# Token routing through expert-sorted DRAM lists in place of one-hot tables, and seven-product arithmetic in all first expert blocks

## The chip, the cores and the metric

The kernel runs on one core of one Trainium2 chip. The metric is the device time of one execution in microseconds (us). A core has a matrix engine (TensorE, PE in the profile; PEld is its weight load), a vector engine (VectorE, DVE), an activation engine (ScalarE, ACT), a general engine (GpSimd, POOL) and a sequencer that issues DMAs (SyncE, SP). Each engine runs its own instruction stream in order and waits on semaphores for the others. In this program the large loads are issued by SP, and the gathers, the scatters and the stores of attention by POOL; all of them share 16 DMA engines.

## The reference

Sliding-window causal attention (8 batches, 8 heads, 576 positions, head size 64, window 64) gives 4608 tokens of 512 features. They go through a mixture of 8 experts with a locality gate, in float32:

```python
logits = x @ w_gate                       # [8, 576, 8]
local_gate = sigmoid(x @ w_local)
for b in range(B):
    prev_e = -1
    for s in range(S):
        fresh_e = argmax(logits[b, s])
        e = fresh_e if s == 0 or local_gate[b, s] < 0.5 else prev_e
        prev_e = e
        p = softmax(logits[b, s])
        h = relu(x[b, s] @ w1[e])         # 512 -> 1024
        out[b, s] = p[e] * (h @ w2[e])    # 1024 -> 512
```

So a token either takes its own best expert or that of the token before it. Which tokens an expert gets is known only once attention is done, and a part of them as soon as the first batches are.

## The kernel before

**Attention** (`attention`, L166) walks over 9 groups of 512 tokens (`sc`), each in 4 head pairs (`hp`): 36 units. A unit is scores (L383), an exponential on ACT (L414), a mask product on DVE (L419), and products with the values (L429), which DVE scales into `x` (L434 to L439). POOL stores `x` to the DRAM tensor `xs` after each group (L529). The gate logits of a group come to `lt`. The order of PE, ACT and SP is the written order here; that of DVE and POOL is chosen by the framework's scheduler. Twice in each unit `step` (L457) takes the next piece of a generator that emits routing work; each piece says by its yield how long it pauses.

**Routing** (`Router`) has two parts. Part 0 is the first three batches (14 chunks of 128 tokens), part 1 the other 23 chunks. `gate` (L766) finds each token's expert by a scan over the tokens, which passes through six small TensorE transposes or sums and back, and ranks the tokens of each expert. Then one-hot tables are built: for each chunk DVE makes `rowh` (128 x 128) and `colh` (128 x 5 x slots) in bf16 (`table`, L926), and one PE product for each chunk (L954) adds them into a table that says, for each slot of 128 rows, which token stands in which row and with what weight. `first` (L970) does part 0 within attention and yields three full blocks of 256 tokens; `second` (L1002) does part 1 after attention.

**Experts** (`Experts.run`, L1402) then works through blocks. `order` has 3 first blocks (-1, -2, -3), 13 blocks of 256 tokens, 4 of 128, 2 of 64 and 2 of 32. `weights` (L1137) reads the block's expert number into a register of SP and loads 2 MB of `w1` and 2 MB of `w2` into a ring of 4 buffers; `rows` (L1114) gathers the block's tokens from `xs` by indirect DMA. `turn` (L1150) transposes the tokens on PE. A *fast* block of 256 tokens uses seven products of quarter matrices instead of eight (`big_hidden` L1192, `big_result` L1244); the sums and differences of quarters that this needs are made on DVE (`left`, `right`, L1171 and L1180): four of `w1`, four of `x`, four of `w2`, four of `h`. Blocks -1 and -2 are listed as `PLAIN` (L73) and take the plain form: L1351 for the hidden layer, L1383 for the result. During these two blocks only PE's order is written out; DVE works off `second`, one piece after some products (`step`, L1417). From block -3 on the order of PE, DVE and ACT is the written one. Block 3 of `order` and all after it depend on `second`.

Of the kernel before, what the change touches and what calls it, by code (L numbers as in the profile page):

```python
# [1 line left out]

# [6 lines left out]
F32 = mybir.dt.float32  # L9
# [25 lines left out]
PIECE = 10  # L35
T1 = 3 * S
CUT = T1 % P
PART = slice(0, T1 // P + 1), slice(T1 // P, C)
C1 = PART[0].stop
CV = C + 1  # L40
CMAX = max(p.stop - p.start for p in PART)
FB = 3
FIRST = 2 * FB
assert CUT and CUT % 32 == 0
LEFT = N - FB * BIG
HF = P // 2
NB = (N + E * (HF - 1)) // BIG
SM0 = NB * 2
HF0 = SM0 + E
NS = HF0 + E  # L50
QR = P // 4
KINDS = NB, NB + E, NB + 2 * E
NBLK = KINDS[-1] + E
SURE = (LEFT + E * HF) // BIG - E // 2, E // 2, E // 4, E // 4
ZR = 16 * P
assert ZR >= T1
# [13 lines left out]
STEP = 3.5  # L70
LEAD = 2
MID = (KB, KB - 1)
PLAIN = (-1, -2)  # L73
# [8 lines left out]
def kernel(  # L82
# [23 lines left out]
    tabs = dict(idx=const.tile([P, NS], U32, name="idx"), pw=const.tile([P, NS], F32, name="pw"),  # L106
                ej=const.tile([1, NBLK + 1], I32, name="ej"), idxh=const.tile([P, E], U32, name="idxh"),
                pwh=const.tile([P, E], F32, name="pwh"),
                idxq=const.tile([P, E], U32, name="idxq"), pwq=const.tile([P, E], F32, name="pwq"), idx1=const.tile([P, FIRST], U32, name="idx1"),
                pw1=const.tile([P, FIRST], F32, name="pw1"), ej1=const.tile([1, FB], I32, name="ej1"),  # L110
                gx=const.tile([P, NS], U32, name="gx"), gx1=const.tile([P, FIRST], U32, name="gx1"))
# [9 lines left out]
    moe = xs, w1, w2, out, tabs, lt, ident  # L121
    with ExitStack() as fast:
        ring = fast.enter_context(tc.tile_pool(name="ring", bufs=4))
        rt = Router(fast, tc, lt, tabs, ident)
# [5 lines left out]
        attention(tc, ring, kq, v3, v4, vt, vh, xs, lt, ok, wgs, wg2s, ident, rt, ex)  # L130
        ex.run(fast, rt, lambda ps: flag(nc, ps, ok, bad, tabs["ej"][:, NBLK:], rare, ident))
    if_rare = nc.values_load(rare[0:1, 0:1], min_val=0, max_val=1,  # L132
                             skip_runtime_bounds_check_because="the larger of two comparisons")
    with tc.If(if_rare > 0):
        if_bad = nc.values_load(bad[0:1, 0:1], min_val=0, max_val=1,
                                skip_runtime_bounds_check_because="the result of a comparison")
        with tc.If(if_bad > 0):
            careful(tc, q, k, v, xs, lt, wgs, ident)
            with ExitStack() as slow:
                ring = slow.enter_context(tc.tile_pool(name="ring2", bufs=4))  # L140
                rt = Router(slow, tc, lt, tabs, ident)
                rt.prepare()
                ex = Experts(slow, tc, ring, *moe)
                with tc.tile_pool(name="rt_ps1", bufs=1, space=PSUM) as ps:
                    for _ in rt.first(lambda: ps.tile([P, SC], F32, name="a")):
                        pass
                ex.begin()
                ex.run(slow, rt)
        if_more = nc.values_load(tabs["ej"][0:1, NBLK:], min_val=0, max_val=1,
# [16 lines left out]
def attention(ctx, tc, ring, kq, v3, v4, vt, vh, xs, lt, ok, wg, wg2, ident, rt, ex):  # L166
# [290 lines left out]
    def step(free=True):  # L457
# [3 lines left out]
        if side and pause <= 0.0 and (free or not trip):  # L461
            w, trip = next(side, (0.0, None))
            pause = max(pause, -HALF) + w
            if trip is None:
                side = ()
                if ex.jobs:
                    ex.rows(ex.jobs[0], -1)
# [1067 lines left out]
```

## Time and profile before

| | |
|---|---|
| three timed runs | 653.6, 653.32, 650.35 us; median 653.32 us |
| the profiled execution | 656.34 us, span of the core 654.3 us |
| granted TensorE clock | 0.994 of full speed |
| busy, share of the span | PE 625.4 us (96%), PEld 538.5 us (82%), DVE 402.2 us (61%), ACT 182.6 us (28%), POOL 124.4 us (19%) |
| DMA | 165.78 MB, 253 GB/s on average |
| attention ends on PE, the first product of block -1 begins | 139.1 us |
| first product of block -3 | 205.1 us |
| first product of the fourth block | 231.9 us |

Times in a profile count from the first instruction of the profiled execution. A row of a timeline gives the start, the time taken, the engine, the line of the kernel and the operation with `out<-in`; in brackets is the time that the engine stood idle before it and who ended the wait. A row of the table of stretches gives the length of a stretch, then the busy time (and instructions) of each engine, the granted clock, the busy share of the DMA engines and the rate.

### The profile page before, as it was taken

What the parts mean: (1) busy time and instruction counts of PE and PEld (TensorE: products, weight loads), DVE (VectorE), ACT (ScalarE), POOL (GpSimd) and SP (SyncE); (2) the same over time, 40 slices, a digit from 0 to 9 for tenths busy, and PEclk for the clock granted to TensorE, in tenths of its full rate; (3) what the DMA queues carried; (4) which work ended last, traced back from release to release, by engine and by line L of the source; (5) the groups of instructions that cost most, each with busy time, mean ns of one, the idle gap of its engine ahead of it and who ended that gap; (6) DMA issues with size and microseconds to landing.
All of it is one profiled execution on the core that took longest, in us unless ns stands there. A gap on an engine that the chain in (4) does not pass through costs nothing. (4 is left out here: it accounts for less than half of the span.)

```text
span 654.3 us, 14680 instructions
## 1 busy us (share of the span) xinstructions
PE 625.4 (96%) x6307; PEld 538.5 (82%) x6307; DVE 402.2 (61%) x742; ACT 182.6 (28%) x318; POOL 124.4 (19%) x131
## 2 busy tenths in 40 slices
PE   8889887999999999999999999999999999999996
PEld 7777765786666899988799799978987998999994
DVE  5676479783996758336290876182835663876730
ACT  2866654621111221203121122113120322123220
POOL 5222111330104111121220311031222111101001
PEclk9999999999999999999999999999999999999998
DMA  9979989997436547566967845686858655945601
GB/s 337 400 292 395 362 311 361 371 357 277 161 128 216 204 160 262 204 218 248 374 244 264 310 174 185 263 304 264 339 183 307 241 198 180 386 165 190 245 17 39
DMA packets 21999, 165.78 MB, mean 253 GB/s; under 512 B 3453, under 2 KB 4483, under 8 KB 11940
## 3 DMA queue, kind: packets, MB, share of 16 engines
q1 hardware_dynamic: 13108, 135.24, 56.7%
q0 software_dynamic: 8816, 29.50, 11.4%
q8 instruction: 52, 0.85, 0.5%
q14 instruction: 23, 0.19, 0.1%
HBM read 145.85 MB, written 19.27 MB: 252 GB/s over the span
## 5 line engine op out<-in xcount | busy, mean ns | idle before, releaser
L1333 POOL DMA_INDIRECT out_dram<-y,idx x36 | 40.4, 1123 | 312.8 <-DVE y L1269 127.9
L1212 PE MATMUL hp<-xs,ws 128*128 128x128 f32 x672 | 79.7, 275 | 1.0 <-issue 1.0
L1212 PEld LDWEIGHTS hp<-xs,ws 128*128 128x128 f32 x672 | 77.3, 192 | 1.2 <-issue 1.2
L1260 PE MATMUL hp<-ws,hs 128*128 128x256 f32 x336 | 77.6, 380 | 0.0
L1260 PEld LDWEIGHTS hp<-ws,hs 128*128 128x128 f32 x336 | 63.5, 190 | 9.3 <-issue 0.8
L1351 PE MATMUL hp<-xt,w 128*64 128x64 f32 (+2 forms) x640 | 65.9, 275 | 0.0
L1269 DVE SCALAR_TENSOR_TENSOR y<-hp,pw,kept 128x256 f32<-128x256 f32 x42 | 19.7, 482 | 73.1 <-issue 48.7
L1351 PEld LDWEIGHTS hp<-xt,w 128*128 128x128 f32 (+1 forms) x640 | 60.8, 170 | 4.6 <-issue 1.1
L1223 DVE TENSOR_TENSOR h<-hp,keep 128x512 f32<-128x512 f32 x42 | 28.6, 690 | 54.0 <-PE hp L1212 46.7
L1131 POOL DMA_INDIRECT xg<-xs,gx x40 | 45.5, 1137 | 84.2 <-PE tp L1157 70.7
L1383 PE MATMUL yp<-w,h 128*128 128x512 f32 x128 | 56.2, 592 | 0.0
L1212 PEld LDWEIGHTS hp<-xt,w 128*128 128x128 f32 x448 | 53.2, 192 | 2.7 <-issue 1.3
L1212 PE MATMUL hp<-xt,w 128*128 128x128 f32 x448 | 54.7, 275 | 0.0
L1260 PE MATMUL hp<-w,h 128*128 128x256 f32 x224 | 53.6, 382 | 0.0
L419 DVE TENSOR_TENSOR p<-p,mask 128x1024 f32<-128x1024 f32 x31 | 39.1, 1265 | 20.7 <-ACT p L414 20.6
L414 ACT ACTIVATE p<-sp 128x512 f32<-128x512 f32 x72 | 39.1, 595 | 41.2 <-PE sp L383 39.1
L383 PEld LDWEIGHTS sp<-w 64*64 64x64 f32 x1296 | 38.7, 138 | 14.1 <-issue 10.7
L429 PE MATMUL xo<-vb,p 128*64 128x74 f32 (+1 forms) x576 | 44.8, 230 | 4.2 <-ACT p L303 1.5
L383 PE MATMUL sp<-w 64*64 64x128 f32 (+1 forms) x1296 | 44.2, 271 | 4.5 <-issue 3.6
L429 PE MATMUL xo<-va,p 128*64 128x74 f32 (+1 forms) x576 | 44.6, 230 | 3.4 <-DVE va L346 3.3
L429 PEld LDWEIGHTS xo<-vb,p 128*64 128x64 f32 x576 | 38.9, 138 | 8.5 <-issue 3.9
L1260 PEld LDWEIGHTS hp<-w,h 128*128 128x128 f32 x224 | 41.3, 190 | 5.6 <-issue 0.4
(284 smaller groups left out, 935.8 us busy)
## 6 DMA issues: line engine op xcount, KB each, us to landing
w<-in_w_dram SPq DMA_DIRECT2D x48, 2048.0 KB, 9.0
w<-in_kq_dram SPq DMA_DIRECT2D x17, 1024.0 KB, 10.5
xs<-x POOLq DMA_DIRECT2D x9, 1024.0 KB
va<-in_v_dram SPq DMA_DIRECT2D x5, 1184.0 KB
vtt<-in_vt_dram SPq DMA_DIRECT2D x5, 1024.0 KB, 6.7
va<-in_v_dram SPq DMA_DIRECT2D x3, 1040.0 KB, 8.0
va<-in_v_dram SPq DMA_DIRECT2D x2, 520.0 KB, 6.9
w<-in_kq_dram SPq DMA_DIRECT2D x2, 512.0 KB, 3.9
```

Of the source, the lines that this page charges most:

```text
L383: nc.tensor.matmul(sp[j][c * WIN:(c + 1) * WIN, a:b], lhsT=kt[h, hp, block * WIN:(block + 1) * WIN], rhs=qt[h, hp, a:b], start=not biased, ...
L414: nc.scalar.activation(p[:, j], sp[j], Act.Exp, scale=DH ** -0.5)
L419: masked.append(nc.vector.tensor_tensor(p, p, m.to_broadcast([P, 2, SC]), op=Alu.mult))
L429: nc.tensor.matmul(xo[par * WIN:(par + 1) * WIN, j, s * VW:s * VW + n], lhsT=p[:, j, b * WIN:(b + 1) * WIN], rhs=w[:, s, 2 * hp + j, :n], ...
L1131: self.nc.gpsimd.indirect_dma_start(out=x, out_offset=None, in_=self.xs[:rows, :], in_offset=bass.IndirectOffsetOnAxis(ap=gx[:, s:s + 1], ...
L1212: nc.tensor.matmul(out[:, m, :], lhsT=a[:, kk, m * P:(m + 1) * P], rhs=b[:, kk, :], start=start and m + kk == 0, stop=stop and (m, kk) == ...
L1223: nc.vector.tensor_tensor(o, x, y, op=add)
L1260: nc.tensor.matmul(out, lhsT=a[:, m, :], rhs=b[:, m, :], start=start and m == 0, stop=stop and m == FK // 2 - 1, skip_group_check=True)
L1269: nc.vector.scalar_tensor_tensor(y[i][:, j * w:(j + 1) * w], x, pw[i], y2, Alu.mult, Alu.add)
L1333: self.nc.gpsimd.indirect_dma_start(out=self.out[:, :], out_offset=bass.IndirectOffsetOnAxis(ap=st["idx"][:, s:s + 1], axis=0), in_=y, in_ ...
L1351: nc.tensor.matmul(hp[a, i, :], lhsT=st["w1"][:, kk, m * P:(m + 1) * P][:, a], rhs=st["xt"][:, kk, :n], start=(kk == 0), stop=(kk == DK - 1))
L1383: nc.tensor.matmul(yp, lhsT=st["h"][:, m, i * P:(i + 1) * P], rhs=st["w2"][:, m, :], start=(m == 0), stop=(m == FK - 1))
```

## The change

The one-hot tables go. Routing now has three parts (tokens to 1728, to 3456 and to 4608: 14, 14 and 9 chunks). At the end of each part's `gate`, every token's number and weight (8 bytes) is written to a row of a DRAM table: a row of its expert's section, at its rank. There are four such tables (`PLANES`), all cleared to zero during attention, and chunk *c* goes to table *c* mod 4 by an indirect DMA from POOL. `listed` works out, for each block, its expert and the row where it begins (16 small DVE operations, three transposes and two more DVE operations), and puts both into a small row that SP can read. `first` is `gate(0)` and `listed` for the first blocks; `rest` is `gate(2)`, 24 small operations and `listed` for all other blocks. For each block, `index` then has SP load the block's rows of all four tables, and `decode` adds the four on DVE (four small operations in all), which gives the token numbers and weights, and issues the gathers. A block of 256 tokens takes 4 such loads of 256 rows, one of 128 takes 4, one of 64 takes 8 and one of 32 takes 16. Part 1's `gate` now runs within attention; part 2's `gate` and the rest of the routing run during the first two blocks.

All three first blocks take the seven-product form; `PLAIN` is gone. Their quarter sums are no longer emitted in one go: `prepare`, `left` and `right` return lists of closures, and the hooks after each product take one or two of them, and then a piece of the routing. In `run` the order of PE, DVE, ACT and SP is the written one from the start. In the diff below, the parts stand in this order: constants, `clear`, the end of `gate`, `listed` and `rest`, `index` and `decode`, `begin`, `big_hidden` (where `after` is called after each of the first six products), and the loop of `run`.

```diff
-PART = slice(0, T1 // P + 1), slice(T1 // P, C)
-PLAIN = (-1, -2)
+ENDS = 3 * S, 6 * S, N
+PART = [slice(a // P, -(-b // P)) for a, b in zip((0, *ENDS), ENDS)]
+PLANES = 4
+ROOM = 0.6
...
+    def clear(self, zeros):
+        self.nc.gpsimd.memset(zeros, 0.0)
+        for t in self.table:
+            self.nc.gpsimd.dma_start(out=t.rearrange("(p r) f -> p (r f)", p=P), in_=zeros)
...
+        vec.tensor_tensor(rank, rank, oh, op=Alu.mult)
+        vec.tensor_reduce(row, rank, axis=AX.X, op=Alu.add)
+        vec.tensor_scalar(pt, row, 0.5, float(2 * ROWS), Alu.is_lt, Alu.mult)
+        vec.tensor_tensor(row, row, pt, op=Alu.add)
+        vec.tensor_copy(row_i, row)
         vec.tensor_tensor(pa, pa, oh, op=Alu.mult)
         vec.tensor_reduce(pt, pa, axis=AX.X, op=Alu.add)
-        vec.tensor_tensor(pt, pt, sm, op=Alu.mult)
+        vec.tensor_tensor(self.field[:, cs, 1], pt, sm, op=Alu.mult)
+        for c in range(n):
+            nc.gpsimd.indirect_dma_start(
+                out=self.table[c % PLANES][:, :], out_offset=bass.IndirectOffsetOnAxis(ap=row_i[:, c:c + 1], axis=0),
+                in_=self.field[:, cs.start + c, :], in_offset=None, bounds_check=NONE - 1, oob_is_err=False)
...
-    def places(self, pl, n):
-    def experts_of(self, ej, n, ends):
-    def table(self, psum, cs, ns, lo, hi, idx, pw, gx):
-    def second(self, psum):
+    def listed(self, many, after, out, more=None):
...
+        ps = self.psum()[:1, :3 * P].rearrange("o (k p) -> o k p", k=3)
+        for k in range(3):
+            self.nc.tensor.transpose(ps[:, k], three[:, k:k + 1], self.ident)
+        vec.tensor_copy(out, ps[:, :2])
...
+    def rest(self):
+        yield from self.gate(2)
...
+        yield from self.listed(many, after, self.lists[1], self.more)
...
+    def index(self, st, n):
+        start = self.value(n, 1, NONE)
+        st["ix"] = ix = self.ip.tile([P, 2, PLANES, 2], F32, name="ix")
+        for k, t in enumerate(self.table):
+            src = t[bass.ds(start, unit), :].rearrange("(s p) f -> p s f", p=rows)
+            for i in range(P // rows):
+                self.nc.sync.dma_start(out=ix[i * rows:(i + 1) * rows, :unit // rows, k, :], in_=src)
+    def decode(self, st):
+        vec.tensor_reduce(jt[:, :s], st["ix"][:, :s].rearrange("p s k f -> p s f k"), axis=AX.X, op=Alu.add)
+...
+        for i in range(s):
+            self.nc.gpsimd.indirect_dma_start(
+                out=x[:n], out_offset=None, in_=self.xs[:rows, :],
+                in_offset=bass.IndirectOffsetOnAxis(ap=gx[:n, i:i + 1], axis=0))
...
     def begin(self):
-        self.jobs = [self.fetch(-1)]
+        self.jobs = [{} for _ in range(FB)]
+        self.weights(self.jobs[0], -1)
+        for i, st in enumerate(self.jobs):
+            self.index(st, -1 - i)
+        self.decode(self.jobs[0])
...
+        if not st["first"]:
+            self.do(more)
+        def after():
+            if st["first"]:
+                self.do(st["sums"], 2) or self.do(more, 1)
+            step()
         product(px, a[0][0], b[0][0], stop=False)
         u = keep(0, px)
+        after()
...
+        self.turn(jobs[0], True)
+        self.do(jobs[0]["sums"], 4)
+        ahead("decode", FB)
+        ahead("weights", FB)
         for i, n in enumerate(order):
+            if i >= FB - 1:
+                ahead("index", i + 4)
+                ahead("weights", i + 3)
+            if i < FB - 1:
+                self.hidden(st, step)
+            elif i == FB - 1:
+                parts = iter([lambda: None, lambda: ahead("decode", FB + 1)])
+                self.hidden(st, lambda: next(parts, lambda: None)())
+            else:
+                self.hidden(st)
+            ahead("decode", i + 4 if i >= FB - 1 else FB)
+            self.turn(after, i + 1 < FB)
+            if i < FB:
+                self.result(st, [lambda: (self.do(after["sums"], 2), step())] * 6)
+            else:
+                self.do(after["sums"])
+                self.result(st)
+            if i == FB - 2:
+                while not over:
+                    step()
```

In `attention`, `begin` is called once `first` is through and group 6 is in its last unit; before, block -1's weights were asked for there and its rows once `first` was through.

## The prediction

> **What bounds the kernel now.** I read the table of stretches first, cut where the first product of block -1, of block -3 and of the fourth block begins. Columns: stretch, its length, then busy us (instructions) of PE, PEld, DVE, ACT, POOL, granted clock, DMA share, GB/s.
>
> ```profile
> 100.00:141.90 41.90, 35.90 (x840) 30.04 (x836) 36.40 (x99) 20.21 (x37) 10.06 (x10) 1.00 0.95 355
> 139.10:205.10 66.00, 63.51 (x260) 42.42 (x257) 51.72 (x134) 9.93 (x17) 10.07 (x9) 1.00 0.56 209
> 205.10:231.90 26.80, 25.80 (x178) 24.17 (x177) 15.87 (x42) 5.64 (x10) 8.55 (x9) 1.00 0.65 228
> 231.90:648.00 416.10, 415.01 (x3149) 372.46 (x3147) 234.92 (x318) 88.06 (x160) 69.08 (x61) 1.00 0.64 234
> ```
>
> From 231.9 us PE idles 1.1 us in 416, so only fewer PE instructions help there, and the change takes none away. From 139.1 to 205.1 PE is full too, but DVE is busy 51.7 of 66 us: that stretch has little DVE time to give. The end of attention has neither: DVE 36.4 of 41.9, DMA 95%. Then the timeline of PE in the two plain blocks and the first fast one (start, time taken, operation, wait before it):
>
> ```profile
> 170.77 13.98 PE L1351 MATMUL hp<-xt,w 128*128 128x256 f32 x64
> ...
> 188.89 2.50 PE L954 MATMUL r<-colh,rowh 128*128 128x270 bf16 x20
> 191.23 10.46 PE L1383 MATMUL yp<-w,h 128*128 128x512 f32 x24
> 201.53 2.15 PE L954 MATMUL r<-colh,rowh 128*128 128x270 bf16 x17
> 205.00 0.27 PE L159 MATMUL r<-ident,ok 128*1 128x128 f32 x1 [1.32 <-DVE t L956]
> ...
> 231.90 1.95 PE L1212 MATMUL hp<-xt,w 128*128 128x128 f32 x16
> ```
>
> and that of DVE beside it: table pieces between the quarter sums of block -3.
>
> ```profile
> 181.88 2.96 DVE L947 TENSOR_TENSOR colh<-one,w 128x2700 bf16<-128x2700 bf16 x1
> ...
> 186.84 0.42 DVE L1185 TENSOR_TENSOR xs<-xt,xs 128x256 f32<-128x256 f32 x1
> ...
> 189.11 1.23 DVE L1177 TENSOR_TENSOR ws<-ws,w 128x1024 f32<-128x1024 f32 x1
> ```
>
> Last, POOL, where one indirect DMA after another starts every 1.3 us:
>
> ```profile
> 141.99 1.01 POOL L1131 DMA_INDIRECT xg<-xs,gx  x1 [0.59 <-DVE pa L786]
> 143.30 1.00 POOL L1131 DMA_INDIRECT xg<-xs,gx  x1 [0.30 <-issue]
> ```
>
> [...] 1.22 us for 1024 elements[...], 0.16 to 0.17 us for 8[...]. So forty small operations cost what six large ones do. [...] block -1's `w2`, issued at 119.7 us, 4.5 us behind `w1`, took 13.0 us to land, against a median of 9.0. [...]
>
> **The change part by part.** The sum is made against the profiled execution: 656.34 us, 2.1 over its span and 3.0 over the median of the timed runs, 653.32.
>
> *PE gains.* A plain block costs 13.8 us (170.77 to the next start at 184.58) and 13.7 us (32 result products at 0.43, 3.43 + 10.3); a fast one seven products at 1.78 us and seven at 1.73, by their starts, 12.5 + 12.1. That is 2.9 us for each, 5.8 for two. L954 goes: 2.34 + 2.15 = 4.5 us. Two waits for DVE go (1.17 at 144.0 and 1.32 above). If PE set the time, block -3 would begin 12 to 13 us earlier, at 192.5.
>
> *But DVE sets it.* DVE work between attention's end and block -3, in program order: quarter sums of `w1` and `w2`, 8 at 1.17 us (spacing of the 1.22 us rows), of `x` 4 at 0.36, of `h` 4 at 0.65: 13.4 us a block, for two blocks 26.8; `w1` and `x` of block -3, 6.1; six sums in `relu` at 0.67 and six in `put` at 0.46, 6.8; `decode` of two blocks, 8 small ones at 0.2, 1.6; `gate(2)`, 39 operations, which took 8.3 us for 14 chunks in `gate(0)` (80 to 100 us) and for 9 chunks some 7.3; `rest` 24 at 0.16 = 3.8; `listed` 18 at 0.19 = 3.4; `flag` 0.6. Sum 56.4 us, against 51.7 busy before.
>
> *When DVE can begin.* Before, it is done with attention at 141.9. `gate(1)` now runs in groups 7 and 8: 8.9 us with 14 chunks, and 1.7 for the row numbers of part 0, 3.4 for `listed`, 0.8 for a `decode`; gone are the first table's pieces between 101.2 and 123.8 us, some 9.6. Net +5.2 us, for which 100 to 141.9 has 5.5 us of idle DVE time, but group 8 (131 to 141) has almost none. I take 2.5 us late: 144.4. PE in attention: about 4.6 us of waits for DVE at 105.6 and 111.6 us may shrink, `gate(1)`'s six round trips cost about 2 and 1.2 MB of clearing (3.4 us at 355 GB/s) meets full DMA engines; I count zero, -4 to +4.
>
> *Waits between DVE and PE.* Part 1's 14 scatters at 1.3 us occupy POOL from about 141 to 159, and the gathers of block -2 queue behind them: 2.6 us and 2.2 to land, 164, while the first hidden layer ends at about 161; 2.5 us, less if the scheduler interleaves them, and then nothing. At the hand-overs from hidden to result DVE waits for the last product and its ReLU, about 0.7 + 0.7; and the last `listed` at the end of block -2 is a chain of DVE, three transposes, DVE, with PE behind it: 2. Sum 6. Block -3 begins at 144.4 + 56.4 + 6 = 206.8, that is **+1.7 us** on 205.1.
>
> *Block -3.* It took 26.8 us. The fourth block's `index` can only start when `listed` is done, at this block's start: [...] four issues at 0.4[...]; `decode`, due after the second product (3.6 us), waits about 1.7 and holds the DVE additions queued behind it, for which PE waits later; `put` waits behind sums, 2. The gathers then land at about 12, when `turn` needs them at 12.5. 24.6 + 0.9 for the turn + 2.5 = 28: **+1.2**.
>
> *After it.* PE's work is the same. Each block adds `decode`, 0.8 us on DVE, hidden by DVE's slack (234.9 of 416 us busy). Its four loads are issued behind the next block's `w2` and must land within the 12.5 us of a hidden layer (7.1 in a block of 128); behind a 9.0 us `w2` they do in the large ones. The size of 8-byte descriptors is not in the trace. [...] SP has 20 us free in each block for its issues. I take **+1.3** for the six small blocks, 0 to +12 as bounds.
>
> Sum +4.2: 660.5 us for its profiled execution, **657.5 us** by the median of the runs.
>
> **The rivals.**
>
> *DVE is not the bound (faster).* Against my sum: DVE idles now in the two plain blocks in several waits of 2 to 3 us for PE, so it has slack that better spacing uses; a piece of routing that comes between products costs PE nothing. It decides if DVE needs less than about 24 us for each of the two blocks, where I have 28. Then block -3 begins 8 to 10 us earlier and the whole gains 6 to 9: about 645 us. For it speaks that table rows of 1.5 to 3 us leave DVE; against it that the two new fast blocks bring 26.8 us of sums.
>
> *Even.* Attention gains the 3 to 4 us of its DVE waits, or the gathers are interleaved: 653, within 3.3 of before.
>
> *The index loads hold DVE in every block (much slower).* Loads that land later than 18 us after a block's start (12.5 and the 5.7 us that DVE has over in a 25.6 us block with 19.9 of DVE work) stop the additions and so PE, at up to 1 us for each us in each of 20 blocks: 668 or more. The largest landing time of the weights before, 16.3 us, says that it can come near, the median that it doesn't.
>
> That the transfers of routing are simply hidden is in all of these; that the seven products aren't made can't be, they are written out.
>
> **How the numbers follow.** Half a per cent, 3.3 us, is about what a measurement tells from no change. My case, DVE-bound, +3.3 to +10: 46%, own range 656.6 to 663. Index loads as bound: 6%. Even: 28%. Faster: 20%. So slower 52%, same 28%, faster 20%. The range for 8 in 10 reaches from 645, the middle of the faster case, to 667, just under the case of the index loads.
>
> **What would show it.** Right: PE idle in 140 to 206 us with waits for DVE (`ws`, `xs`, `hs`), DVE over 85% busy there, block -3's first product at 205 to 209, PE full from about 236. Wrong: DVE with gaps there and block -3 at 197 or earlier; attention ending later than 143 (clearing or scatters in its way); PE waits after 240 us; PE waiting for `xg` before the fourth block.

## The result and the profile after

The changed kernel takes 713.31 us (median of four runs, three of them from 712.0 to 713.4), the kernel before took 653.46 us beside it (650.35 to 654.05): a ratio of 1.092, 95% interval 1.0875 to 1.0965. The change costs 9%, some 60 us. The profiled execution took 713.26 us, its span is 711.5 us and the mean granted clock 0.947. The fourth run of the changed kernel (1276.1 us) and one of the first attempt with scatters alone (681.3 us) were much slower than the others of the same kernel, and no reading below rests on them.

This is where the span grew, by the same cuts as in the prediction:

| | before, us | after, us | difference |
|---|---|---|---|
| first product of block -1 (attention's end on PE) | 139.1 | 176.7 | +37.6 |
| from there to the first product of block -3 | 66.0 | 77.9 | +11.9 |
| from there to the fourth block | 26.8 | 25.8 | -1.0 |
| fourth block to the last product | 415.9 | 420.5 | +4.6 |
| last product to the end of the span | 6.5 | 10.7 | +4.2 |

PE's busy time rose by 8.1 us only (625.4 to 633.5), its idle time by 49.1. The table of stretches of the changed kernel, with the columns of the prediction's first fence (stretch, length, busy us of PE, PEld, DVE, ACT, POOL, granted clock, DMA share, GB/s):

```profile
100.00:176.70 76.70, 49.71 (x932) 40.26 (x925) 40.65 (x135) 22.73 (x41) 24.95 (x23) 0.77 0.81 253
176.70:254.60 77.90, 58.70 (x368) 52.82 (x368) 55.85 (x153) 15.22 (x28) 40.14 (x31) 0.88 0.41 92
254.60:280.30 25.70, 25.66 (x177) 23.89 (x177) 19.70 (x39) 5.67 (x10) 9.16 (x7) 1.00 0.78 286
280.30:700.00 419.70, 415.73 (x3143) 373.79 (x3144) 240.79 (x390) 87.85 (x159) 67.58 (x64) 1.00 0.67 234
```

In the first stretch no engine is full: PE 49.7 of 76.7 us, DVE 40.7, and the DMA engines move 253 GB/s where they moved 355 before. In the second DVE has the 56 us of work that was forecast, but 78 us to do it in. From the fourth block on the picture is that of before.

The timeline of PE in the changed kernel, the rows with the long waits (start, time taken, operation, wait and who ended it):

```profile
62.67 1.56 PE L386 MATMUL sp<-w 64*64 64x128 f32 x26 [6.83 <-ACT p L417]
122.73 0.23 PE L432 MATMUL xo<-va,p 128*64 128x74 f32 x1 [3.10 <-issue]
132.73 0.80 PE L948 MATMUL r<-ident,three 128*1 128x128 f32 x3 [3.60 <-DVE va L349]
160.97 0.77 PE L871 MATMUL r<-oh,ones 128*128 128x112 f32 x2 [8.55 <-DVE oh L863]
169.77 1.08 PE L1089 MATMUL tp<-ident,xg 128*128 128x128 f32 x4 [4.04 <-DMA xg<-xs,ji]
173.38 0.69 PE L1089 MATMUL tp<-ident,xg 128*128 128x128 f32 x2 [2.53 <-DMA xg<-xs,ji]
209.43 0.90 PE L1089 MATMUL tp<-ident,xg 128*128 128x128 f32 x3 [13.92 <-DMA xg<-xs,ji]
```

Most of them go back to a transfer. At 62.67 PE waits for ACT, which waits for one of the five `p` buffers of attention: the zeros of `clear` lie in one, and their stores, issued at 45 us, ran from 51.5 to 61.0 us behind a store of `x`. At 132.73 it waits for DVE's part of `va`, which comes after ACT's part of `vb`, for which ACT waited 3.3 us until POOL's copy of 130.12 (below) was done. At 122.73 the profile names nobody (`issue`), and the products with `va` in this unit had begun before; the last section comes back to it. At 160.97 it waits for DVE, which stood at the first block's index. In the DVE timeline of the same kernel:

```profile
157.86 0.17 DVE L1044 TENSOR_REDUCE jt<-ix 128x4 f32<-128x16 f32 x1 [7.12 <-DMA ix<-table]
```

At 169 and 173 PE waits for the gathers of block -1 (`xg`), with the last products of attention behind them in its order. At 209 it waits 13.9 us for those of block -2. The POOL timeline shows both rows of scatters (L907), in attention and in block -1:

```profile
128.69 1.45 POOL L907 DMA_INDIRECT table<-field,row_i  x1 [0.30 <-issue]
130.12 1.20 POOL L366 COPY vb<-va 64x1184 f32<-64x1184 f32 x1
135.77 0.99 POOL L907 DMA_INDIRECT table<-field,row_i  x1 [4.46 <-DMA table<-field,row_i]
...
188.49 1.68 POOL L1062 DMA_INDIRECT xg<-xs,ji  x1 [0.30 <-issue]
...
198.64 1.72 POOL L1062 DMA_INDIRECT xg<-xs,ji  x1 [0.30 <-issue]
```

Part 0's fourteen scatters take POOL from 106 to 139 us; the copy at 130.12 stands behind twelve of them. Part 1's take it from 180 to 214, and the two gathers of block -2 stand among them.

Last, the row of the page that gives the granted TensorE clock, in 40 slices of the span:

```profile
PEclk9997997785869999999999999999999999999997
```

and the same row of the kernel before:

```profile
PEclk9999999999999999999999999999999999999998
```

Between 59 and 213 us the clock was at half for 65 us in all, in eight stretches of 3.4, 6.8, 10.2 or 13.7 us; between the same points of the kernel before it was one stretch of 3.4 us. In the 3.4 us ahead of each of the eight PE was busy for 0 to 1.54 us, so idle for more than half of them. That took no long wait: ahead of the half speed at 110.3 us PE was busy for 1.5 of the 3.4 us, and no wait was longer than 1.1 us. Products are slower there: eight of L1219 took 3.08 us at 210.34 us, with the clock at half up to 212.7, and 1.89 us at 213.26. So most of the long waits are paid a second time, in slow products after them. By the prediction's count seven-product blocks and the missing L954 took 10.3 us of products away, and yet PE's busy time rose by 8.

### The profile page after: what moved, and what is told of

Read it like the earlier page. It is cut to its first block, busy times and chain, and to the rows that moved or that the text cites. A ratio compares the mean times of both kernels' runs of the same rounds, so it can differ in the third digit from the quotient of the medians.

```text
span 711.5 us, 15657 instructions
## 1 busy us (share of the span) xinstructions
PE 633.5 (89%) x6416; PEld 558.9 (79%) x6416; DVE 418.5 (59%) x862; ACT 187.8 (26%) x329; POOL 173.3 (24%) x180
## 3 DMA queue, kind: packets, MB, share of 16 engines
q1 hardware_dynamic: 35636, 135.41, 54.9%
q0 software_dynamic: 10160, 30.08, 12.8%
## 5 line engine op out<-in xcount | busy, mean ns | idle before, releaser
L1289 POOL DMA_INDIRECT out_dram<-y,ji x38 | 42.3, 1114 | 269.2 <-DVE y L1228 87.7
L1153 PE MATMUL hp<-xs,ws 128*128 128x128 f32 x768 | 92.7, 278 | 1.9 <-DVE xs L1119 1.9
L1153 PEld LDWEIGHTS hp<-xs,ws 128*128 128x128 f32 x768 | 90.0, 195 | 2.1 <-issue 2.1
L1219 PE MATMUL hp<-ws,hs 128*128 128x256 f32 x384 | 89.3, 380 | 2.0 <-issue 2.0
L1219 PEld LDWEIGHTS hp<-ws,hs 128*128 128x128 f32 x384 | 72.4, 190 | 13.2 <-issue 3.6
L1119 DVE TENSOR_TENSOR ws<-w 128x1024 f32<-128x1024 f32 x64 | 77.8, 1216 | 7.8 <-PE hp L1219 7.8
L1062 POOL DMA_INDIRECT xg<-xs,ji x40 | 45.0, 1125 | 119.9 <-DVE xt L1090 53.1
L1153 PE MATMUL hp<-xt,w 128*128 128x128 f32 x512 | 65.0, 282 | 2.5 <-issue 2.5
L1228 DVE SCALAR_TENSOR_TENSOR y<-hp,jt,kept 128x256 f32<-128x256 f32 x48 | 22.7, 482 | 71.3 <-PE hp L1219 45.0
L1219 PE MATMUL hp<-w,h 128*128 128x256 f32 x256 | 62.3, 387 | 0.0
L1119 DVE TENSOR_TENSOR ws<-w,ws 128x1024 f32<-128x1024 f32 x48 | 58.6, 1221 | 0.5
L907 POOL DMA_INDIRECT table<-field,row_i x37 | 45.7, 1234 | 38.2 <-DMA table<-field,row_i 17.6
L1219 PEld LDWEIGHTS hp<-w,h 128*128 128x128 f32 x256 | 48.2, 194 | 6.6 <-issue 0.4
```

Of the source, the lines that this page charges most:

```text
L907: nc.gpsimd.indirect_dma_start(out=self.table[c % PLANES][:, :], out_offset=bass.IndirectOffsetOnAxis(ap=row_i[:, c:c + 1], axis=0), in_=s ...
L1062: self.nc.gpsimd.indirect_dma_start(out=x[:n], out_offset=None, in_=self.xs[:rows, :], in_offset=bass.IndirectOffsetOnAxis(ap=gx[:n, i:i + ...
L1119: return lambda: self.nc.vector.tensor_tensor(o, x, y, op=op)
L1153: nc.tensor.matmul(out[:, m, :], lhsT=a[:, kk, m * P:(m + 1) * P], rhs=b[:, kk, :], start=start and m + kk == 0, stop=stop and (m, kk) == ...
L1219: nc.tensor.matmul(out, lhsT=a[:, m, :], rhs=b[:, m, :], start=start and m == 0, stop=stop and m == FK // 2 - 1, skip_group_check=True)
L1228: nc.vector.scalar_tensor_tensor(y[i][:, j * w:(j + 1) * w], x, pw[i], y2, Alu.mult, Alu.add)
```

## The experiments

Two theories stood against each other. *Late transfers*: the new small DMAs (clearing, scatters, index loads, gathers) and what stands behind them in the queues of POOL, DVE and PE make PE wait. *DVE's work*: the prediction's own, quarter sums and routing fill DVE. (Four of the expectations call them the round-trip theory and the DVE-load theory.) In the diffs, the lines are those of the changed kernel unless said otherwise. Four groups follow: one suspect at a time in the changed kernel, one half of the change at a time, the scatters alone in the kernel before, and repairs. A result without an interval is that of a single execution. Where there were two of one kernel, they differed by up to 6.2 us, so a smaller difference of totals says little without its trace.

### One suspect at a time

**Zeros of their own.**

```diff
-rt.clear(pp.tile([P, 2, SC], F32, name="p").rearrange("p i q -> p (i q)")[:, :CLEAR])
+rt.clear(cp.tile([P, CLEAR], F32, name="zeros"))
```

> The changed kernel with one edit: the zeros that clear the four tables lie in a tile of their own and not in one of the five buffers of attention's probabilities. Round-trip theory (the loss is made of waits for the new DMAs, in attention above all): the 6.8 us wait of PE near 62 us goes, and with it the half-clock stretch after it; unit (3,0) comes 8 to 9 us earlier, and of this 4 to 9 us stay to the end: 704 to 709 us. DVE-load theory (the prediction's: quarter sums and routing fill DVE before block -3): no change, 711 to 715 us.

Measured: 707.71 us, 5.6 less. The wait of 6.83 us at 62.67 is gone, and the clearing is issued at 16 us. Group 5's products with values begin at 89.0 us, level with the kernel before (89.8), where the changed kernel is at 94.4: up to there the borrowed buffer was the cost, and not the 1.2 MB, which are stored here too. The gain does not come where it was forecast, though: the unit (3, 0), the first of group 3, begins 4.5 us later than in the changed kernel, and group 4 is the first to gain. And a later wait grows: at 132.88 PE stands 15.5 us for `va`, where it stood 3.6.

**Index loads ahead of the weights.**

```diff
-self.weights(self.jobs[0], -1)
 for i, st in enumerate(self.jobs):
     self.index(st, -1 - i)
+self.weights(self.jobs[0], -1)
```

> The changed kernel with the loads of the lists of the first three blocks issued before the 4 MB of weights of block -1. Round-trip theory: the lists land 5 us or more earlier, so DVE's wait of 7.1 us for them at 150 us shrinks to under 3 and PE's wait behind it from 8.5 to under 4; the weights come later by some us and may take a part back; 700 to 710 us. DVE-load theory: 711 to 715 us.

Measured: 704.2 us, 9.1 less, inside what late transfers foretold. Block -1 begins at 166.7. But the wait did not shrink as foretold. The list is there 11 us earlier, and DVE stands for it longer than before, with PE 9.4 us behind it:

```profile
146.66 0.17 DVE L1044 TENSOR_REDUCE jt<-ix 128x4 f32<-128x16 f32 x1 [10.12 <-DMA ix<-table]
```

**One scatter for each part.**

```diff
-for c in range(n):
+for c in range(1):
     nc.gpsimd.indirect_dma_start(out=self.table[c % PLANES][:, :], ...
```

> The changed kernel with 1 instead of 14, 14 and 9 scatters after each part of gate, so that most tokens are missing from the lists and their rows are taken from the zero row and not stored; the blocks, their experts and all arithmetic stay. Round-trip theory: POOL is free, the value copies and gathers come on time, the wait of 13.9 us for block -2's gather is under 3 us and attention ends 15 to 20 us earlier; 675 to 690 us. DVE-load theory: DVE has the same work, block -3 starts no more than 5 us earlier, 706 us or more.

Measured: 677.04 us, 36.3 less. All of DVE's work is still there (419.4 us busy, 418.5 in the changed kernel), so DVE's work is not what took 60 us. PE's wait for the gathers of block -2 is gone. Block -1 begins at 161.0, block -3 at 221.3 (60 us later, against 77.9 in the changed kernel).

**All three together.** 

> The changed kernel with zeros of their own, index loads ahead of the weights, and one scatter for each part (most rows of the result are not stored). Everything else, all DVE work with it, stays. Late transfers: 655 to 668. DVE's work: 672 or more.

Measured: 667.2 us, ratio to before 1.0215 (1.0167 to 1.0263), at the upper end of the first forecast. So 46 of the 60 us go with the transfers, 14 do not. The 46 are an upper bound for scatters, loads and clearing: as most rows of the result are not stored, POOL's queue also moves 8.8 MB less (21.28 in place of 30.08). Its table of stretches, cut as above:

```profile
100.00:145.40 45.40, 34.68 (x757) 29.18 (x758) 34.69 (x101) 19.05 (x34) 9.77 (x9) 0.89 0.79 267
145.40:210.50 65.10, 57.08 (x369) 52.11 (x368) 55.73 (x156) 15.07 (x28) 13.41 (x10) 0.95 0.48 168
210.50:237.60 27.10, 25.95 (x178) 23.91 (x178) 19.70 (x39) 5.67 (x10) 9.32 (x7) 1.00 0.70 257
```

With the transfers out of the way DVE is 86% busy in the two first blocks, and they take 65 us: no less than the 66 of before, although PE has 10.3 us less to do in them. Here the prediction's bound comes close. Of the 8.0 us that PE is idle in them, though, 3.3 us are at 164.86 for DVE, which itself stood 2.9 us for a store of `x`. Attention's end stays 6.3 us late.

**The same, with part 1's gate in the blocks.**

```diff
-stages = [(PART[0].stop, rt.first), (PART[1].stop, lambda: rt.gate(1))]
+stages = [(PART[0].stop, rt.first)]
 ...
-return side
+return rt.gate(1)
```

> The same as i3_clear_way, but the second part's gate (8.9 us of DVE work and six round trips between DVE and PE) runs in blocks -1 and -2 in place of the end of attention. If DVE is the bound in these blocks: what attention gains is lost again there, within 3 us of i3_clear_way or slower. If DVE has room there: attention's end comes 4 to 8 us earlier and the whole is 3 to 8 us faster.

Measured: 679.1 us, ratio to before 1.0397 (1.0359 to 1.0434), 11.9 more than with the three edits together. Attention now ends at 138.6 us, as before the change, so this gate and its round trips cost attention 6.8 us. But the blocks lose more. The table of stretches, and then the timelines of PE and DVE:

```profile
138.60:221.05 82.45, 58.20 (x376) 51.50 (x377) 63.40 (x187) 14.25 (x28) 12.02 (x11) 0.88 0.41 154
221.05:249.20 28.15, 28.11 (x178) 26.32 (x178) 19.70 (x39) 5.67 (x10) 7.67 (x6) 0.91 0.77 265
```

```profile
218.68 0.37 PE L948 MATMUL r<-ident,three 128*1 128x128 f32 x1 [9.60 <-DVE past L937]
```

```profile
157.71 0.69 DVE L1164 TENSOR_TENSOR h<-hp,keep 128x512 f32<-128x512 f32 x1 [7.17 <-DMA xs<-x]
```

DVE's work rose by 7.7 us and the stretch by 17.3. What is left of the routing runs bare just ahead of block -3's start: a chain of some 60 small DVE operations, with PE behind it for 9.6 us. It isn't that DVE lacks time (63 of 82 us): the pieces that are handed out between products are too few, and the rest stands in a row. But a part of the growth is a transfer again: at 161 us PE waits 7.9 us (3.3 with the three edits together) for DVE, which stands until a store of `x` has landed. So "DVE's work" is right about the place and about a part of the loss, and it acts as a chain, not as a full engine.

### One half of the change at a time

**The new routing with plain blocks -1 and -2.** The plain hidden layer and result of the kernel before, put into the changed kernel:

```diff
+PLAIN = (-1, -2)
 ...
+        if st["plain"]:
+            return self.plain_hidden(st, step)
         if st["big"]:
             return self.big_hidden(st, step)
```

> The changed kernel, with its routing, but blocks -1 and -2 at eight products each, as before. The sums of those two blocks on DVE (26.8 us and the adds) are not made, PE has 5.8 us more to do. Late transfers: PE has slack in waits anyway, 710 to 720. DVE's work: 700 or less.

Measured: 718.7 us, ratio to before 1.1003 (1.0972 to 1.1035), inside the first forecast. So the routing with plain blocks costs 65.5 us, 5.4 more than the whole change. That difference is not PE's 5.8 us by count, but the rest of two larger ones. The stretches from block -1 to -3 and from there to the fourth block:

```profile
177.43:243.45 66.02, 61.65 (x223) 40.59 (x223) 22.46 (x102) 9.81 (x17) 27.83 (x28) 0.97 0.44 108
243.45:283.99 40.54, 31.85 (x177) 29.21 (x177) 19.73 (x39) 5.63 (x10) 11.23 (x10) 0.83 0.57 202
```

The first is 11.9 us shorter than in the changed kernel. Without the sums DVE decodes block -2's index at 161 us, still in attention, its gathers go out at 176.9 us, ahead of part 1's scatters, and the wait of 13.9 us is not there; in the changed kernel that decoding comes at 182.7 us, behind four of the sums. So the place of the decoding has its part in that wait. The second stretch is 14.7 us longer: SP begins the fourth block's index loads 7.7 us after block -3 (0.3 in the changed kernel), and DVE waits 9.4 us for them.

**The old routing with seven products in all first blocks.** In the kernel before; the routing's pieces are handed out after each product.

```diff
-STEP = 3.5
+STEP = 1.75
 ...
-PLAIN = (-1, -2)
+PLAIN = ()
 ...
```

> The kernel before with one part of the change alone: blocks -1 and -2 in seven products, their quarter sums before each hidden layer, routing by one-hot tables as it was, its pieces taken after each product. Round-trip theory: the seven products are not the loss; DVE gets 21 us of sums more in a stretch with 14 us of idle time, so 650 to 660 us. DVE-load theory: 665 us or more.

Measured: 671.2 us, 20 more than the 651.1 of before beside it, so the forecast from DVE's work was the right one here. Its stretches from block -1 to -2 and from -2 to -3, and PE's timeline:

```profile
133.30:180.40 47.10, 31.32 (x191) 28.39 (x188) 35.11 (x108) 7.10 (x13) 4.73 (x5) 0.86 0.44 167
180.40:221.70 41.30, 33.33 (x215) 28.94 (x214) 40.85 (x67) 7.59 (x14) 5.78 (x3) 0.92 0.44 159
```

```profile
148.17 1.19 PE L1212 MATMUL hp<-xs,ws 128*128 128x128 f32 x4 [12.77 <-DVE ws L1177]
```

Block -2's stretch has DVE busy 40.9 of 41.3 us: there sums and one-hot tables fill it. In block -1's it is not full, and of the 12.8 us wait DVE itself stood idle 7.7 for something that the profile doesn't name. With tables on DVE and the pieces in this order the seven products don't pay.

**The same for block -2 alone.**

```diff
-PLAIN = (-1, -2)
+PLAIN = (-1,)
 ...
```

> The kernel before with its one-hot tables, and block -2 alone by seven products (block -1 stays at eight, its table pieces in their old places). PE has 2.9 us less to do. If it was the sums at attention's end, in front of block -1, that cost the version with three fast blocks its 12.8 us wait: 650 to 655, from 3 us faster to 2 slower. If DVE is too full with tables for any more sums: 657 or more.

Measured: 671.3 us (668.1 and 674.4), ratio 1.0289 (1.0147 to 1.0432). The second forecast holds: leaving block -1 plain gives nothing back. PE waits 4.9, 3.8, 2.6 and 2.2 us for DVE between 158 and 233 us.

### The scatters alone, in the kernel before

**First attempt.**

> The kernel before, untouched in its routing, with fourteen scatters of 8-byte rows added in attention at the place where the first part's stand in the changed kernel (four small tables cleared beforehand from zeros of their own). Nobody reads what they store. If the row of scatters on POOL holds the copies of vb, and so va and PE: 8 to 15 us more than before, 661 to 668. If only what is built on them (index, gathers) or DVE's work costs: within 3 us of before.

Measured: 669.9 us in the profiled run. But the row numbers were ready at the start, and the scheduler put the scatters at 21 to 50 us, ahead of the first copies of `vb` (35.1 us, 18.1 before); there attention lost 12 to 16 us. It shows the cost of such a row on POOL, not at the place in question.

**With index loads.**

> The same, and twelve index loads of 256 rows behind the first weights, with one sum on DVE that reads the first block's. Gathers and everything else stay those of before. If DVE's wait for the index holds attention: 6 to 12 us more than with the scatters alone. If the loads are hidden: within 3 us of it.

Measured: 685.3 us, ratio 1.0505 (1.0416 to 1.0593). The scatters stand at the start here too. SP spent 17.1 us to issue the twelve loads of 8-byte rows, and attention lost 5 us after them. Its start differs from that of the first attempt by 9 us, so the difference of the two totals says nothing of the loads.

**At their place.**

```diff
+        if (sc, hp) == (5, 3):
+            nc.vector.tensor_scalar(late, allr[:, 5, 2, 0, 0:1], 0.0, None, Alu.mult)
+            nc.vector.tensor_scalar(row_f, fields, 1.0, late, Alu.mult, Alu.add)
+            nc.vector.tensor_copy(row_u, row_f)
+            for c in range(14):
+                nc.gpsimd.indirect_dma_start(
+                    out=ex.table[c % 4][:, :],
+                    out_offset=bass.IndirectOffsetOnAxis(ap=row_u[:, c:c + 1], axis=0),
...
```

> The kernel before with fourteen scatters whose row numbers depend on a reciprocal of group 5, so that they stand on POOL in the changed kernel's order, four, a copy of vb, four, a store of x, four, a copy, two. No clearing, and nobody reads what they store (the earlier version, whose row numbers were ready at the start, had them run at 21 to 50 us). If the row of scatters on POOL holds the copies: 8 to 15 us more than before, 660 to 667, and PE waits for va at 115 to 135 us. If not: within 4 us of before.

Measured: 674.3 us against 653.15, ratio 1.0323 (1.0293 to 1.0353): 21 us for fourteen scatters of 1 KB that nobody reads. Attention's end is 15.3 us later, and 3.3 us more come after the last product. The POOL timeline, then a row of DVE and one of PE:

```profile
121.39 1.55 POOL L526 DMA_INDIRECT table<-fields,idx  x1 [0.30 <-issue]
122.92 1.21 POOL L365 COPY vb<-va 64x1184 f32<-64x1184 f32 x1
136.77 1.90 POOL L526 DMA_INDIRECT table<-fields,idx  x1 [12.64 <-DMA table<-fields,idx]
138.97 1.94 POOL L526 DMA_INDIRECT table<-fields,idx  x1 [0.30 <-issue]
140.91 1.19 POOL L361 COPY vb<-va 64x1184 f32<-64x1184 f32 x1
```

```profile
135.28 0.69 DVE L441 TENSOR_TENSOR x<-xo,allr 128x512 f32<-128x512 f32 x1 [6.71 <-DMA xs<-x]
```

```profile
136.03 0.38 PE L431 MATMUL xo<-vb,p 128*64 128x74 f32 x1 [4.29 <-DVE x L441]
```

The thirteenth scatter waits 12.6 us until an earlier one into its table has landed, and two copies of `vb` stand behind it. The stores of `x` (1 MB each) are in the same POOL queue: that of group 5 is issued at 116.4, between scatters (at 106.9 before), and DVE waits for it until 135 before it may write the `x` of group 7. The loss is larger than forecast, and its path is another one: PE waits only 0.6 us for `va`, and its longest wait, the 4.3 us above, leads by way of DVE to the store. Its busy time rises too, since 10.2 us of attention run at half clock. Copies, stores and scatters hold each other up.

**Each into a table of its own.**

```diff
-out=ex.table[c % 4][:, :]
+out=ex.table[c][:, :]
```

> The kernel before with the same fourteen late scatters as in i1_scatters_late, each into a table of its own, so that none has to wait until an earlier one has landed. If the waits for landing (up to 12.6 us for one pair there) hold the copies of vb behind them: all fourteen are issued within some 18 us, and the cost falls from 21 us to 10 or less. If POOL's own time for the fourteen, or their 1792 small packets among attention's transfers, is the cost: 17 us or more stay.

Measured: 673.4 us (670.4 and 676.3), ratio 1.0333 (1.0227 to 1.0440): as much as with the waits, as the second forecast has it. The scatters do go out within 21 us, but in one piece, so that the store and all four copies come after them. POOL, DVE and PE:

```profile
120.30 1.90 POOL L526 DMA_INDIRECT table<-fields,idx  x1 [0.30 <-ACT p L416]
122.19 0.82 POOL L546 DMA_DIRECT2D xs<-x  x1
123.01 1.18 POOL L361 COPY vb<-va 64x1184 f32<-64x1184 f32 x1
```

```profile
140.95 0.69 DVE L441 TENSOR_TENSOR x<-xo,allr 128x512 f32<-128x512 f32 x1 [11.21 <-DMA xs<-x]
```

```profile
141.69 0.39 PE L431 MATMUL xo<-vb,p 128*64 128x74 f32 x1 [6.40 <-DVE x L441]
```

The loss is therefore there without the waits for landing. What they cost by themselves isn't shown, as the order on POOL changed with the edit. In both runs the row of scatters in front of copies and stores is on PE's path; how much is POOL's 1.3 us for each and how much the transfers' own delay isn't separated by these runs.

### Repairs in the changed kernel

Each of these has zeros of their own.

**Only block -1's index early.**

```diff
-        self.weights(self.jobs[0], -1)
-        for i, st in enumerate(self.jobs):
-            self.index(st, -1 - i)
+        self.index(self.jobs[0], -1)
+        self.weights(self.jobs[0], -1)
 ...
-        at = dict(index=FB, weights=1, decode=1)
+        at = dict(index=1, weights=1, decode=1)
 ...
+        ahead("index", FB)
```

> The changed kernel with zeros of their own for the clearing, and with only block -1's four index loads in the start of the experts, ahead of its weights (the other two blocks' loads come after attention). If late transfers set the time: the wait for ix on DVE in attention shrinks from 7 to under 2 us, block -1's gathers land before PE asks for them, the first product of block -1 comes at 155 to 165 us, and the whole takes 690 to 702. If DVE's own work set it, nothing of that work is less: 705 to 709, as with the zeros alone (707.7).

Measured: 714.15 us, a miss for both theories. Attention's end did come 17 us earlier (159.5), but the loads of blocks -2 and -3 now stand behind part 1's scatters into the same tables. SP, DVE and PE:

```profile
188.58 4.80 SPq L1037 DMA_DIRECT2D ix<-table  x8
```

```profile
192.34 0.17 DVE L1044 TENSOR_REDUCE jt<-ix 128x4 f32<-128x16 f32 x1 [26.40 <-DMA ix<-table]
```

```profile
199.87 0.60 PE L824 MATMUL r<-ident,vk 128*9 128x128 f32 x2 [28.22 <-DVE vk L817]
```

DVE's order is written out: one operation that waits for a load holds sums, ReLU and routing behind it, and PE stands 28 us.

**The same, block -1 decoded after attention.**

```diff
-        self.decode(self.jobs[0])
 ...
+        ahead("decode", 1)
         self.turn(jobs[0], True)
```

> The same as f1_lean, but what DVE and POOL do with block -1's index (the sums of its planes and the gathers) is written after attention, so that no instruction of attention stands behind it on DVE. If it is DVE's wait for the index in attention that costs: as f1_lean or up to 5 us less, 687 to 702. If the gathers' landing is what counts, they now start later and PE stands bare before block -1: 5 to 10 us more than f1_lean.

Measured: 717.6 us, 3.4 more than the repair before it, between the two forecasts. Attention's wait did not go: the scheduler put the decoding ahead of attention's last operations all the same, DVE stood 9.6 us for the index up to 144.7 and PE 9.0 behind it. Block -1 begins 12 us later (171.9), of which most is given back, since the scatters of part 1 are awaited afterwards anyway.

**The same as the first, scatters two at a time.**

```diff
+            if c % 2:
+                yield 0.6, False
 ...
```

> The same as f1_lean, and the scatters of a part come two at a time, with other work of the kernel written between each pair, in place of fourteen in a row. If the queue of scatters on POOL holds the copies of vb and the gathers: 8 to 15 us less than f1_lean, 678 to 692, and the wait of 14 us for block -2's gathers gone. If only the landing of the last scatter matters, it is no faster than f1_lean or slower, since the last scatter then comes later. If DVE's work sets it: as f1_lean.

Measured: 704.7 us, 9.4 less than the first repair, as forecast, but from a higher start, so 13 over the upper end. There is no long wait for block -2's gathers, but there was none in the first repair either; what is gone is its wait of 28.2 us. The last scatter comes later, and with it the fourth block's index: PE waits 4.1 us for the list and 6.0 for the gathers.

**The same as the first, one scatter for each part.**

> The same as f1_lean with one scatter for each part, in place of 14, 14 and 9; most tokens' entries are not stored, so most rows of the blocks are the zero row and the result lacks them, while every instruction of DVE and PE stays. It shows what is left when neither scatters nor crowded loads hold anything. Late transfers: 655 to 665 (677.0 with few scatters alone, less 5 for the zeros and 8 to 12 for the loads). DVE's work: 672 or more.

Measured: 673.15 us, above the late-transfer forecast: block -2's index, still read after part 1's one scatter, holds DVE 7.2 us and PE 10.4.

**Zeros, index order and spread scatters.**

> The changed kernel with three of the separate edits together: zeros of their own for the clearing, the three blocks' index loads ahead of block -1's weights, and scatters two at a time. Late transfers: the gains of the three partly add (5.6 and 9 measured alone), 685 to 697. DVE's work: 700 to 709.

Measured: 701.4 us (699.6 and 703.1), ratio 1.0751 (1.064 to 1.0861). A miss: the gains don't add. DVE now stands 9.2 us in block -1 until a store of `x` has landed:

```profile
179.22 0.69 DVE L1166 TENSOR_TENSOR h<-hp,keep 128x512 f32<-128x512 f32 x1 [9.16 <-DMA xs<-x]
```

**Zeros, index order, copies of `vb` on ACT.**

```diff
-        nc.gpsimd.tensor_copy(vb[:WIN, :2], va[:WIN, :2])
+        copy = nc.scalar.copy if sc >= 7 else nc.gpsimd.tensor_copy
+        copy(vb[:WIN, :2], va[:WIN, :2])
```

> The changed kernel with zeros of their own, the index loads ahead of the weights, and the copies of vb for groups 7 and 8 on ACT, away from POOL and its scatters. If the copies behind the scatters are what costs attention most: 688 or less, 12 us or more under the two edits without it (about 700). If the last landing (index, gathers) decides: 697 or more.

Measured: 701.1 us (700.0 and 702.3), ratio 1.0760 (1.0718 to 1.0802), so the second forecast holds. Attention is level with the kernel before at the start of group 7 (118.2 us), where the changed kernel is 17 us behind, and then loses all of it within two units: group 8 begins at 152.8 us, 2.8 us later than in the changed kernel. DVE's timeline shows why:

```profile
130.94 0.69 DVE L443 TENSOR_TENSOR x<-xo,allr 128x512 f32<-128x512 f32 x1 [9.25 <-DMA xs<-x]
141.63 0.17 DVE L1045 TENSOR_REDUCE jt<-ix 128x4 f32<-128x16 f32 x1 [10.00 <-DMA ix<-table]
```

First the store behind the scatters, then the index behind the last of them. Then PE waits 13.1 us for the gathers of block -2. Copies, store, index and gathers lie one behind the other; taking one wait away bares the next. No version with all its scatters came near the kernel before.

## Why the prediction was wrong

**The direction was right, the size wrong by a factor of fourteen.** Forecast was 657.5 us, measured 713.3; the range ended at 667.

**The step that failed is "PE in attention: ... I count zero, -4 to +4".** It was +37.6 us. Of its terms: the clearing was priced by its bytes, while its cost was the `p` buffer (5.6 us in a single run); `gate(1)`'s round trips were put at 2 us of PE, and without this gate attention ends 6.8 us earlier. The largest term was missing: part 0's fourteen scatters in attention. The prediction counted scatters on POOL only for part 1, and asked only which gathers stand behind them. The copies of `vb` and the stores of `x`, in the same queue, were not asked about; alone they make fourteen scatters cost 15 us of attention. Nor was the order of DVE and PE carried into attention's end: a `decode` that waits for its loads stands on DVE ahead of attention's own operations, and a `turn` on PE ahead of attention's last products.

**"Waits between DVE and PE", 2.5 us for block -2's gathers,** had the mechanism and missed the size: 13.9 us. POOL was indeed taken by part 1's scatters, but from 180 to 214 us, since each took 1.0 to 2.5 us and some waited for others to land (up to 3.7 us); and the gathers stood among them, after a decoding that came later than the first scatters.

**"But DVE sets it"** had the work right, 56.4 us, where the profile shows 55.85 (2.4 of them still attention's last operations, which the prediction had put ahead of its sum). As a bound it comes close only once the transfers are out of the way: then the two blocks take 65.1 us, near the 62.4 that the prediction gave from DVE's start. In the changed kernel DVE waits there. The forecast of DVE over 85% busy in these blocks is wrong for it (72%).

**PE's gains** were right as a count: block -2's hidden layer takes 12.5 us (224.7 to 237.2) where a plain one took 13.8. That the version with plain blocks is 5.4 us slower, near the 5.8 of the count, is luck: two shifts of 12 and 15 us nearly cancel there.

**Block -3** was forecast at +1.2 and came at -1.0: DVE waited 0.9 us for the fourth block's index, where 1.7 was forecast (the times of SP's register load and of the landing in it were the author's estimates, which no run had shown), and no wait of PE followed from it.

**"After it", +1.3 with bounds 0 and 12,** was +4.6: in one block near the end (614 us) DVE stands 5.3 us for its index, with the copies of the next `xt` behind it, and PE 2.5 us behind those, with 3.4 us of half clock after it; 1.5 us are waits of PE in the results ahead of small blocks. What the 8-byte packets would take was the author's estimate, which no run had shown; measured, they took 8.9 ns of a DMA engine's time each. The 4.2 us after the last product were in no step.

**The rivals.** "Index loads hold DVE in every block" came nearest in time, and its mechanism was at work, but in the wrong place: DVE waited for index loads seven times, 18.0 us in all, the 7.1 us in attention and the 5.3 near the end with PE behind them, the other five 0.5 to 2.2 us each. None of the cases had attention itself as the place of a loss, though the list of what would prove the prediction wrong did ("attention ending later than 143"). The range was too narrow because a term with three unknown transfers in full DMA engines was given 8 us in all.

**What stays open.** Of the 14 us that are left with the three edits together, attention's 6.3 fit the gate, and 3.8 after the fourth block lie in four waits of PE (0.7, 0.7, 1.4 and 1.0 us). The two profiled executions differ by 9.8 us only, so the other 4 are difference between executions. How POOL's own time and the transfers' delay share attention's loss, and what a decoding of block -2 ahead of the sums would give, no run shows.

## What to carry to other kernels

The small indirect DMAs of this kernel cost what stood behind them in their engine's queue, not what their bytes took: list every copy, store and gather of that engine near the new ones, and who needs each. Where an engine's order is written out, an operation that waits for a chain of transfers (scatter, load, sum, gather) must not stand in front of work that was ready; move the start of the chain, not its last link. And a gain measured with one wait removed doesn't show what is gained without its neighbours: here several waits were in line. Nor is a difference of two totals the price of the part that was exchanged, until the stretches agree.

## What the runs showed of the hardware

- Fourteen scatters of 128 rows of 8 bytes took 8.6 to 10.5 us to land, median 9.9, in `k1_own_tables`, among attention's loads and stores of about 1 MB each.
- The last drain of POOL grows with the DMAs that POOL has issued in the whole kernel: 0.81 us after 93 (the kernel before), 1.21 after 100, 1.95 after 107, 2.27 after 111, 4.15 after 134 (the changed kernel, and the same in every run of 134), and an instruction ahead of it from 0.38 to 1.20 us between 93 and 134. That is 4.2 us for this change's 41, 0.1 us for each, at the very end where nothing hides it.
- SP's queue has 22,500 packets more (35,636 against 13,108), 20,480 of them the index loads' of 8 bytes, at 8.9 ns each in the engines; the time of the whole queue in the engines rises by 14 ns for each packet more. What shows beside that is their issue: SP took 13.6 us for twelve loads of 2 KB in the changed kernel's attention, and 17.1 us in the kernel before with scatters and index loads.
- PE's waits that the profile puts down to `issue` have a common mark in attention: over all 20 traces there are 51 above 0.8 us, and 45 of them end 1.2 to 1.6 us after a packet of 16 KB has landed on the queue that the profile's page calls `instruction` (q8), though the moments at that distance from such a packet make up under 6% of attention's time. The 3.1 us at 122.73 us are one of them, 1.2 us after a packet. What these packets bring, and whether PE waited for them, no run shows.
